# Middle tokens' output made transposed, and last block's slots 8, 9 and 11 through the common block routine

## The chip, the cores and the metric

One NeuronCore of a Trainium2 chip runs the whole kernel in one launch. The metric is the device time in microseconds (us) of one execution; the time of a kernel is the median of several executions. Engines: TensorE (PE in the profile; PEld is its weight load), VectorE (DVE), ScalarE (ACT), GpSimd (POOL), and SyncE (SP), which here only issues DMAs. PSUM is the memory that TensorE writes; DVE and ACT read it, in banks of 128 partitions x 512 fp32.

## The reference

`x` is (8, 3072, 256): 8 batches of 3072 tokens with 256 features. Two Fourier transforms (over tokens, over features), the real part, then a feed-forward layer with a maximum of three projections:

```python
X = np.fft.fft(x, axis=1)
X = np.fft.fft(X, axis=2)
x = X.real.reshape(8 * 3072, 256)
h = np.maximum(np.maximum(x @ w1, x @ w2), x @ w3)      # 768 wide
out = h @ w_out                                         # (24576, 256), float32
```

## The kernel before

**What is computed together.** The real part of the transform of a real sequence has a symmetry: token n and its mirror token 3072 - n are made of the same two parts, an even one `tE` and an odd one `tO`, by their sum and difference. So the kernel computes `tE` and `tO` (bf16, features on partitions) for half of the tokens, 1536 per batch, and makes two outputs of each: "plus" and "minus". Token 1536 is its own mirror; these 8 middle tokens, one per batch, are kept in `t_mid` (128 features x 2 parts x 8).

**The feed-forward part.** `max(a, b, c) = a + max(0, b - a, c - a)`. The term `a` is linear, so its product with `w_out` is folded into one small matrix `gw`: columns 0 to 255 for the even part, 256 to 511 for the odd one, 512 a marker column, and 514 to 769 the odd one with the signs of the mirrored half. Layer 1 (`unit_plus`, `unit_minus`, `unit_out`) makes the hidden values `hp` (plus) and `hm` (minus), 768 wide, as 6 chunks `jc` of 128; layer 2 multiplies them by `wout_bf`.

**Tiles and stages.** A batch has 3 blocks of 512 half tokens; a block is 6 layer-1 units (one per `jc`) and 4 slots of 128 half tokens, so a batch has slots 0 to 11. Partition p of slot s is the token with row r + 24p, r = s + 1, and its mirror is row 24 - r - 24p counted from the end. Slot 11 (r = 12) is its own partner row and needs special ranges.

**Order.** All engine orders are written out by hand (a manual schedule): the order of the calls is the order on each engine. Layer 1 of a block runs beside layer 2 of the block before: `l2_some(n)` takes n steps of the generator at the head of `l2_queue`, some 9 matmuls per unit. Behind each unit `l2_odd` is called for a slot whose line is ready, if fewer than two banks are in use.

**Layer 2 of an ordinary block** (`l2_even`, `l2_odd`, `l2_block`, lines 623 to 691). `l2_even` makes the even products of two slots in one PSUM bank `pl` (L629) and ScalarE copies them to an SBUF tile `even` (L632); the dictionary `lines` holds, for each slot, its part of `even`. `l2_odd` makes the odd product in a bank `po` (L640; pool `ps_o` has two such banks), DVE computes `other` from it (L643), the odd part with its sign turned, and POOL adds it to the even part (L646), which gives the line of the minus half. `odd` holds the bank, `banks` the slots in use. `l2_block` then accumulates 6 hidden products for plus and 6 for minus on the same bank (`l2_hidden`, L616), pops the slot's `lines` and `odd` before that, and adds line and bank on DVE (L670) into an output tile `ot` (4 buffers). Two slots share one `ot` up to slot 9. The minus half goes out by an indirect DMA from POOL (L677, rows from the table `rows_m`), since its rows run backwards; the plus half by a DMA from SP (L689).

**Layer 2 of the very last block** (batch 7, slots 8 to 11; `l2_last`, lines 693 to 728). There both halves are made from scratch: for each of the slots 11, 8, 9, 10 and each half, an even product (L711), an odd product (L713) and 6 hidden products, 16 matmuls per slot. The minus half uses tokens turned round, so that its rows run forwards and plain stores suffice: POOL turns `tE` and `tO` into `tEr` and `tOr` (L909, 512 columns each), and DVE writes the last block's `hm` backwards (`finish`, L891 to 894). DVE copies each bank out (L719, or L717 by halves for slot 10). Ten stores follow: nine from SP and one from ScalarE's queue (L727).

**Middle tokens** (`l2_mid`, lines 730 to 759). It runs beside block 0 of batch 7, five steps per unit. Layer 1 uses `t_mid` as 8 moving columns (L739, L741), layer 2 as 8 stationary columns: two products with `gw` (L752) and six with `wout_bf` (L616), each 256 columns wide, into 8 partitions of a bank `pom`; DVE copies 8 x 256 (L757) and SP stores 8 rows of 1 KB (L758).

Of the kernel before, what the change touches and what calls it, by code (L numbers as in the profile page):

```python
# [33 lines left out]
def kernel(  # L34
# [585 lines left out]
    odd = {}  # L620
    banks = set()

    def l2_even(b, slot):

        pl = ps_f.tile([128, 512], FP32, name="pl", tag="ps")
        for i in range(2):
            ci = (slot + i) * 128
            yield
            nc.tensor.matmul(pl[:, i * 256:(i + 1) * 256], mixes[b].tE[:, ci:ci + 128],  # L629
                             gw[:, 0:256], start=True, stop=True)  # L630
        even = even_pool.tile([128, 1024], FP32, name="even", tag="even")
        nc.scalar.copy(out=even.rearrange("p (i c) -> p i c", i=2)[:, :, 0:256],  # L632
                       in_=pl.rearrange("p (i c) -> p i c", i=2))
        for i in range(2):
            lines[b, slot + i] = even[:, i * 512:(i + 1) * 512]

    def l2_odd(b, slot):
# [12 lines left out]
    def l2_block(b, blk, hp, hm):  # L650

        base = b * S
        for sub in range(4):
            slot = blk * 4 + sub
            r = slot + 1
            sp = slice(sub * 128, sub * 128 + 128)
            if sub % 2:
                after = (b, slot + 1) if slot < 11 else (b + 1, 0)
                if after < (B - 1, 8):
                    yield from l2_even(*after)  # L660
            lin = lines.pop((b, slot))
# [8 lines left out]
            nc.vector.tensor_tensor(out=parts, in0=po.rearrange("p (i c) -> p i c", i=2),  # L670
                                    in1=lin.rearrange("p (i c) -> p i c", i=2), op=ALU.add)
            banks.remove((b, slot))
            if pair and not sub % 2:
                continue
            place = b * 7 + (slot // 2 if pair else slot - 5)
            wide = 512 if pair else 256
            stored(nc.gpsimd.indirect_dma_start(  # L677
                out.rearrange("(n two) c -> n (two c)", two=2) if pair else out,
                bass.IndirectOffsetOnAxis(ap=rows_m[:, place: place + 1], axis=0),
                ot[:, wide:2 * wide], None), "scattered", ("scattered", "direct"))  # L680
            nc.gpsimd.memset(mark, 0.0)
            if pair:
                stores = [(0, 128, base + r - 1)]
            elif r == 11:
                stores = [(0, 128, base + r)]
            else:
                stores = [(1, 64, base + 24), (64, 128, base + 12)]
            for (p0, p1, row) in stores:
                stored(nc.sync.dma_start(  # L689
                    out=bass.AP(out.tensor, out.offset + row * 256, [[24 * 256, p1 - p0], [1, wide]]),  # L690
                    in_=ot[p0:p1, 0:wide]), "direct", ("scattered",))

    def l2_last(hp, hm, te, to, flipped):

        base = (B - 1) * S
        ter, tor = flipped
        for sub in (3, 0, 1, 2):
            slot = 8 + sub
            r = slot + 1
            cp = slice(slot * 128, slot * 128 + 128)  # L700
            sp = slice(sub * 128, sub * 128 + 128)
            sm = slice((3 - sub) * 128, (4 - sub) * 128)
            po = ps_o.tile([128, 512], FP32, name="po", tag="po")
            ot = out_pool.tile([128, 1024], FP32, name="ot", tag="ot")
            for (h, tev, tov, wo, hid) in (
                    (0, te[:, cp], to[:, cp], gw[:, 256:512], lambda jc: hp[:, jc, sp]),
                    (1, ter[:, sm], tor[:, sm], gw[:, 514:770], lambda jc: hm[:, jc, sm])):
                if sub == 2 and h == 1:
                    po = ps_f.tile([128, 512], FP32, name="pol", tag="ps")
                ph = po[:, h * 256:(h + 1) * 256]  # L710
                nc.tensor.matmul(ph, tev, gw[:, 0:256], start=True, stop=False)  # L711
                yield
                nc.tensor.matmul(ph, tov, wo, start=False, stop=True)  # L713
                yield
                yield from l2_hidden(ph, hid)
                if sub == 2:
                    nc.vector.tensor_copy(out=ot[:, h * 256:(h + 1) * 256], in_=ph)  # L717
            if sub != 2:
                nc.vector.tensor_copy(out=ot[:, 0:512], in_=po)  # L719
            if r <= 11:  # L720
                stores = [(0, 128, base + r, 0), (0, 128, base + 24 - r, 256)]
            else:
                stores = [(0, 64, base, 0), (64, 128, base + 12, 0),
                          (0, 64, base + 1548, 256), (64, 127, base + 1560, 256)]
            for k, (p0, p1, row, c) in enumerate(stores):
                eng = nc.scalar if sub == 2 and k == 0 else nc.sync
                stored(eng.dma_start(out=out[row: row + 24 * (p1 - p0 - 1) + 1: 24, :],  # L727
                                     in_=ot[p0:p1, c:c + 256]), "direct", ("scattered",))

    def l2_mid():  # L730

        hmid = h_pool.tile([128, NJC, B], BF16, name="hmid", tag="hmid")
        n = NJC * B
        psm = ps_f.tile([128, 512], FP32, name="psm", tag="ps")
        for i in range(2):
            for jc in range(NJC):
                js = slice(jc * 128, (jc + 1) * 128)
                cs = slice(i * n + jc * B, i * n + (jc + 1) * B)
                nc.tensor.matmul(psm[:, cs], gE[i][:, js], t_mid[:, 0, :],  # L739
                                 start=True, stop=False)  # L740
                nc.tensor.matmul(psm[:, cs], gO[i][:, js], t_mid[:, 1, :],  # L741
                                 start=False, stop=True)
                yield
        stmp = h_pool.tile([128, TOKB + 16], BF16, name="stmp", tag="stmp")
        nc.scalar.activation(out=stmp[:, 0:n], in_=psm[:, 0:n], func=AX.Relu)
        nc.vector.tensor_tensor(out=hmid.rearrange("p jc n -> p (jc n)"), in0=psm[:, n:2 * n],
                                in1=stmp[:, 0:n], op=ALU.max)
        po = ps_f.tile([128, 512], FP32, name="pom", tag="ps")
        for _ in range(6):
            yield  # L750
        for k in range(2):
            nc.tensor.matmul(po[0:B, 0:256], t_mid[:, k, :], gw[:, k * 256:(k + 1) * 256],  # L752
                             start=(k == 0), stop=(k == 1))
            yield
        yield from l2_hidden(po[0:B, 0:256], lambda jc: hmid[:, jc, :])
        ot = out_pool.tile([128, 1024], FP32, name="ot", tag="ot")
        nc.vector.tensor_copy(out=ot[0:B, 0:256], in_=po[0:B, 0:256])  # L757
        stored(nc.sync.dma_start(out=out[NHALF: NHALF + S * (B - 1) + 1: S, :],  # L758
                                 in_=ot[0:B, 0:256]), "direct", ("scattered",))

    l2_queue = []

# [123 lines left out]
    for b in range(B):  # L886
# [4 lines left out]
        def finish(prev):  # L891
            pses, to, jc, hm = prev
            unit_minus(pses, to, jc)
            unit_out(pses, hm[:, jc, ::-1] if hm is last_hm else hm[:, jc, :], TOKB)

        last_hm = None
        if b == B - 1:
            flipped = []
            for t, name in ((tE, "tEr"), (tO, "tOr")):
                fl = h_pool.tile([128, TOKB], BF16, name=name, tag=name)  # L900
                flipped.append(fl)
        for blk in range(3):
            cs = slice(blk * TOKB, (blk + 1) * TOKB)
            hp = h_pool.tile([128, NJC, TOKB], BF16, name="hp", tag="hp")
            hm = h_pool.tile([128, NJC, TOKB], BF16, name="hm", tag="hm")
            if b == B - 1 and blk == 2:
                last_hm = hm
                for t, fl in zip((tE, tO), flipped):
                    nc.gpsimd.tensor_copy(fl, t[:, 3 * TOKB - 1: 2 * TOKB - 1: -1])  # L909
            for jc in range(NJC):  # L910
                pses = unit_plus(tE[:, cs], tO[:, cs], jc, TOKB)
                unit_out(pses, hp[:, jc, :], TOKB)
# [15 lines left out]
            l2_some(1000)  # L928
            if blk == 2:
                finish(prev)  # L930
            l2_queue.append(l2_last(hp, hm, tE, tO, flipped) if b == B - 1 and blk == 2 else
                            l2_block(b, blk, hp, hm))

    l2_some(1000)

# [28 lines left out]
```

## Time and profile before

| what | value |
|---|---|
| time, median of 3 runs (lowest, highest) | 405.08 us (404.48, 406.48) |
| profiled execution: its time | 406.24 us |
| profiled execution: span, first to last instruction | 404.5 us |
| granted TensorE clock | 1.00 in all 40 slices |
| hidden products L616, `hp` and `hm` | 1146 records, 171.2 us |
| layer-1 matmuls L591, L592, L599 | 816 records, 287.2 us |
| DVE add L670 | 92, mean 682 ns |
| DVE `other` L643 | 92, mean 476 ns |
| POOL add of even and other L646 | 92, mean 764 ns |
| POOL indirect store L677 | 53, mean 1018 ns |
| hardware queue q1 | 101976 packets, 42.21 MB, 41.9% of 16 DMA engines' span |

How to read it: the span is a little shorter than the time of the same execution, since it leaves out what lies before the first and behind the last instruction. A line of the timeline gives start, duration, engine, line of the code, operation, output <- inputs with their shapes, how many were merged, and in brackets how long the engine had been idle and what released it. Matmul durations overlap: a row of six matmuls of 0.273 us each takes 0.82 us. "SPq" and "ACTq" are DMA issues.

### The profile page before, as it was taken

How to read it: one execution, taken by the hardware profiler on the slowest of the kernel's cores; microseconds unless marked ns; L12 is line 12 of the kernel's file. 1: busy time of each engine (PE TensorE's matmuls, PEld its weight loads, DVE VectorE, ACT ScalarE, POOL GpSimd, SP SyncE). 2: the span in 40 equal slices, each digit the busy share in tenths (PEclk: the TensorE clock that was granted, in tenths of full speed). 3: DMA queues.
4: the chain of work that ended last, by engine and by line, in shares of the span. 5: the costliest groups of instructions: out<-in, count | busy, mean ns of one | idle time of the engine just before them, and what ended most of it. 6: DMA issues, size and time to landing. Idle time of an engine off the chain costs nothing.

```text
span 404.5 us, 8566 instructions
## 1 busy us (share of the span) xinstructions
PE 387.4 (96%) x2832; PEld 261.1 (65%) x2880; DVE 309.7 (77%) x556; ACT 265.5 (66%) x489; POOL 291.9 (72%) x394
## 2 busy tenths in 40 slices
PE   0999999999999999999999999999999999999996
PEld 0455677766676666766667666766677676666665
DVE  8798776787776886787777887778777877678884
ACT  6778667656766567666766676666766577655550
POOL 9589879879987898778967898768967623323521
PEclk9999999999999999999999999999999999999999
DMA  9999797689778848786489818886234411211214
GB/s 116 209 167 184 153 231 195 156 213 191 197 184 213 195 126 206 200 180 180 119 199 217 191 68 211 211 180 192 74 111 111 124 55 64 94 52 54 105 55 156
DMA packets 127598, 62.06 MB, mean 153 GB/s; under 512 B 111617, under 2 KB 116737, under 8 KB 126977
## 3 DMA queue, kind: packets, MB, share of 16 engines
q1 hardware_dynamic: 101976, 42.21, 41.9%
q0 software_dynamic: 24640, 18.98, 22.9%
q8 instruction: 22, 0.36, 0.4%
q10 hardware_dynamic: 936, 0.33, 0.3%
q14 instruction: 24, 0.19, 0.2%
HBM read 33.74 MB, written 29.88 MB: 157 GB/s over the span
## 4 chain that ended last, share of the span: by engine, by line
PE 88%; DVE 6%; issue 3%; ACT 2%; DVEq 0%; POOL 0%; ACTq 0%; POOLq 0%
PE po L616 29%; PE pse L591 16%; PE pse L599 14%; PE pse L592 12%; PE ps L571 3%; PE ps L573 3%; PE po L640 3%; PE pl L629 2%; PE warm L773 2%; PE ps L547 2%; DVE hm L606 2%; ACT stmp L605 2%; DVE other L643 1%; DVE ot L670 1%; PE psw L509 0%
## 5 line engine op out<-in xcount | busy, mean ns | idle before, releaser
L605 ACT ACTIVATE stmp<-pse 128x512 bf16<-128x512 f32 x288 | 170.7, 600 | 52.6 <-PE pse L592 26.1
L606 DVE TENSOR_TENSOR hp<-pse,stmp 128x512 bf16<-128x512 f32 x144 | 99.5, 691 | 80.3 <-ACT stmp L605 52.4
L646 POOL TENSOR_TENSOR even<-even,other 128x256 f32<-128x256 f32 x92 | 70.3, 764 | 76.3 <-DVE other L643 76.0
L591 PE MATMUL pse<-t,gE 128*128 128x512 bf16 x288 | 109.2, 379 | 2.6 <-DVE gD L488 0.2
L606 DVE TENSOR_TENSOR hm<-pse,stmp 128x512 bf16<-128x512 f32 x144 | 99.1, 689 | 3.3 <-ACT stmp L605 3.1
L592 PE MATMUL pse<-t,gO 128*128 128x512 bf16 x249 | 94.3, 379 | 0.0
L616 PE MATMUL po<-wout_bf,hp 128*128 128x256 bf16 x576 | 85.9, 272 | 0.0
L616 PE MATMUL po<-wout_bf,hm 128*128 128x256 bf16 x570 | 85.3, 273 | 0.3
L599 PE MATMUL pse<-t,gD 128*128 128x512 bf16 x279 | 83.7, 379 | 0.1
L677 POOL DMA_INDIRECT out_dram<-ot,rows_m x53 | 54.0, 1018 | 20.1 <-DVE ot L670 10.7
L616 PEld LDWEIGHTS <-hp 128*128 128x128 bf16 x576 | 56.3, 98 | 17.3 <-issue 2.5
L616 PEld LDWEIGHTS <-hm 128*128 128x128 bf16 x576 | 56.3, 98 | 16.6
L670 DVE TENSOR_TENSOR ot<-po,even 128x512 f32<-128x512 f32 x92 | 62.7, 682 | 0.0
L172 POOL CAST xw<-xs 96x544 bf16<-96x544 f32 (+1 forms) x48 | 53.3, 1122 | 0.0
L177 POOL CAST xb<-xs 96x512 bf16<-96x512 f32 x48 | 52.6, 1101 | 0.0
L575 ACT CAST t<-ps 128x512 bf16<-128x512 f32 x48 | 27.9, 586 | 34.8 <-PE ps L573 34.7
L599 PEld LDWEIGHTS <-gD 128*128 128x128 bf16 x288 | 28.1, 98 | 32.2
L643 DVE SCALAR_TENSOR_TENSOR other<-twice,po 128x256 f32<-128x256 f32 x92 | 43.8, 476 | 0.1
L591 PEld LDWEIGHTS <-gE 128*128 128x128 bf16 x288 | 28.2, 98 | 20.1 <-issue 0.7
L592 PEld LDWEIGHTS <-gO 128*128 128x128 bf16 x288 | 28.1, 98 | 20.1 <-issue 1.8
L552 ACT CAST z_all<-ps 128x480 bf16<-128x480 f32 x46 | 24.8, 560 | 23.2 <-PE ps L547 23.1
L632 ACT COPY even<-pl 128x512 f32<-128x512 f32 x46 | 27.0, 588 | 9.7 <-PE pl L629 8.6
(178 smaller groups left out, 373.3 us busy)
## 6 DMA issues: line engine op xcount, KB each, us to landing
xs<-in_x_dram SPq DMA_DIRECT2D x84, 198.0 KB
out_dram<-ot SPq DMA_DIRECT2D x39, 256.0 KB
xs<-in_x_dram SPq DMA_DIRECT2D x28, 192.0 KB
held<-xb SPq DMA_DIRECT2D x48, 96.0 KB
xw<-held POOLq DMA_DIRECT2D x24, 192.0 KB
raw_w<-in_moe_w_dram SPq DMA_DIRECT2D x4, 384.0 KB
out_dram<-ot SPq DMA_DIRECT2D x12, 128.0 KB
x<-in_x_dram POOLq DMA_DIRECT2D x8, 120.0 KB
```

Source lines behind the costliest of these rows:

```text
L172: nc.gpsimd.tensor_copy(v[:, d0:d1, ch * 32:ch * 32 + 32], xs[:, 0:32 * 64].rearrange("p (bb dl) -> p dl bb", dl=64)[:, d0:d1, :])
L177: nc.gpsimd.tensor_copy(mir[:, d0:d1, c0:c0 + 32], bass.AP(xs.tensor, xs.offset + 33 * 64 - 1 - d0, [xs.ap[0], [-1, d1 - d0], [-64, 32]]))
L591: nc.tensor.matmul(pse[:, 0:n], gE[i][:, js], te, start=True, stop=False)
L592: nc.tensor.matmul(pse[:, 0:n], gO[i][:, js], to, start=False, stop=True)
L599: nc.tensor.matmul(pse, gD[i][:, js], to, start=False, stop=True, skip_group_check=True)
L605: nc.scalar.activation(out=stmp[:, 0:n], in_=pses[0][:, 0:n], func=AX.Relu)
L606: nc.vector.tensor_tensor(out=dst, in0=src3, in1=stmp[:, 0:n], op=ALU.max)
L616: nc.tensor.matmul(po, hcols(jc), wout_bf[:, jc * 256:(jc + 1) * 256], start=False, stop=(jc == NJC - 1), skip_group_check=True)
L643: nc.vector.scalar_tensor_tensor(out=other, in0=twice, scalar=po[:, 256:257], in1=po[:, 0:256], op0=ALU.mult, op1=ALU.subtract)
L646: nc.gpsimd.tensor_tensor(out=line[:, 256:512], in0=line[:, 0:256], in1=other, op=ALU.add)
L670: nc.vector.tensor_tensor(out=parts, in0=po.rearrange("p (i c) -> p i c", i=2), in1=lin.rearrange("p (i c) -> p i c", i=2), op=ALU.add)
L677: stored(nc.gpsimd.indirect_dma_start(out.rearrange("(n two) c -> n (two c)", two=2) if pair else out, bass.IndirectOffsetOnAxis(ap=rows_m ...
```

## The change

Three parts.

- `l2_mid`: layer 2 uses `gw` and `wout_bf` as stationary (128 columns) and the 8 tokens as moving columns, in two halves of the 256 features: 16 matmuls into `pom` (128 features x 16). DVE copies 128 x 16. Two DMAs store it, each with 128 x 8 runs of one element.
- The last block goes through `l2_block` for slots 8, 9 and 11, with `l2_even` (slot 11 alone by `which=(1,)`), `l2_odd` called from inside the loop, and indirect stores for the minus half. `l2_last` is left with slot 10.
- Only slot 10 is turned round: two copies of 128 columns of `tE`, `tO` into `tEr`, and behind each unit of the last block one copy of 128 columns of `hm` by POOL, into `tOr` (chunks 0 to 3) or `tEr` (chunks 4, 5). `hm` itself is written forwards.

```diff
-    def l2_even(b, slot):
+    def l2_even(b, slot, which=(0, 1)):
         pl = ps_f.tile([128, 512], FP32, name="pl", tag="ps")
-        for i in range(2):
+        for i in which:
...
-        nc.scalar.copy(out=even.rearrange("p (i c) -> p i c", i=2)[:, :, 0:256],
-                       in_=pl.rearrange("p (i c) -> p i c", i=2))
-        for i in range(2):
+        i0, i1 = which[0], which[-1] + 1
+        nc.scalar.copy(out=even.rearrange("p (i c) -> p i c", i=2)[:, i0:i1, 0:256],
+                       in_=pl.rearrange("p (i c) -> p i c", i=2)[:, i0:i1, :])
+        for i in which:
             lines[b, slot + i] = even[:, i * 512:(i + 1) * 512]
...
     def l2_block(b, blk, hp, hm):
         base = b * S
-        for sub in range(4):
+        at_end = (b, blk) == (B - 1, 2)
+        for sub in (0, 1, 3) if at_end else range(4):
             slot = blk * 4 + sub
+            for more in (slot, slot + 1 if sub < 1 else 11) if at_end else ():
+                if (b, more) in lines and len(banks) < 2:
+                    l2_odd(b, more)
             r = slot + 1
...
                 after = (b, slot + 1) if slot < 11 else (b + 1, 0)
-                if after < (B - 1, 8):
+                if after < (B - 1, 10):
                     yield from l2_even(*after)
+                elif after == (B - 1, 10):
+                    yield from l2_even(*after, (1,))
             lin = lines.pop((b, slot))
             po = odd.pop((b, slot))
...
-    def l2_last(hp, hm, te, to, flipped):
+    def l2_last(hp, te, to, flipped):
         base = (B - 1) * S
-        ter, tor = flipped
-        for sub in (3, 0, 1, 2):
...
+        ter, tor, hidden_r = flipped
+        cp = slice(10 * 128, 11 * 128)
+        ot = out_pool.tile([128, 1024], FP32, name="ot", tag="ot")
+        for (h, tev, tov, wo, hid) in (
+                (0, te[:, cp], to[:, cp], gw[:, 256:512], lambda jc: hp[:, jc, 256:384]),
+                (1, ter, tor, gw[:, 514:770], hidden_r)):
+            pool, name, tag = ((ps_o, "po", "po"), (ps_f, "pol", "ps"))[h]
+            po = pool.tile([128, 512], FP32, name=name, tag=tag)
+            ph = po[:, 0:256]
+            nc.tensor.matmul(ph, tev, gw[:, 0:256], start=True, stop=False)
+            yield
+            nc.tensor.matmul(ph, tov, wo, start=False, stop=True)
+            yield
+            yield from l2_hidden(ph, hid)
+            nc.vector.tensor_copy(out=ot[:, h * 256:(h + 1) * 256], in_=ph)
+        for (eng, row, c) in ((nc.scalar, base + 11, 0), (nc.sync, base + 13, 256)):
+            stored(eng.dma_start(out=out[row: row + 24 * 127 + 1: 24, :], in_=ot[:, c:c + 256]),
+                   "direct", ("scattered",))
...
     def l2_mid():
...
-        for k in range(2):
-            nc.tensor.matmul(po[0:B, 0:256], t_mid[:, k, :], gw[:, k * 256:(k + 1) * 256],
-                             start=(k == 0), stop=(k == 1))
-            yield
-        yield from l2_hidden(po[0:B, 0:256], lambda jc: hmid[:, jc, :])
+        for half in range(2):
+            to_bank = po[:, half * B:(half + 1) * B]
+            for k in range(2):
+                c = k * 256 + half * 128
+                nc.tensor.matmul(to_bank, gw[:, c:c + 128], t_mid[:, k, :],
+                                 start=(k == 0), stop=False)
+            for jc in range(NJC):
+                c = jc * 256 + half * 128
+                nc.tensor.matmul(to_bank, wout_bf[:, c:c + 128], hmid[:, jc, :],
+                                 start=False, stop=(jc == NJC - 1))
+                if jc % 2:
+                    yield
         ot = out_pool.tile([128, 1024], FP32, name="ot", tag="ot")
-        nc.vector.tensor_copy(out=ot[0:B, 0:256], in_=po[0:B, 0:256])
-        stored(nc.sync.dma_start(out=out[NHALF: NHALF + S * (B - 1) + 1: S, :],
-                                 in_=ot[0:B, 0:256]), "direct", ("scattered",))
+        nc.vector.tensor_copy(out=ot[:, 0:2 * B], in_=po[:, 0:2 * B])
+        for half in range(2):
+            stored(nc.sync.dma_start(
+                out=bass.AP(out.tensor, out.offset + NHALF * 256 + half * 128,
+                            [[1, 128], [S * 256, B], [1, 1]]),
+                in_=ot[:, half * B:(half + 1) * B].unsqueeze(2)), "direct", ("scattered",))
...
         def finish(prev):
             pses, to, jc, hm = prev
             unit_minus(pses, to, jc)
-            unit_out(pses, hm[:, jc, ::-1] if hm is last_hm else hm[:, jc, :], TOKB)
+            unit_out(pses, hm[:, jc, :], TOKB)
+            if hm is last_hm:
+                nc.gpsimd.tensor_copy(last_hidden(jc), hm[:, jc, 383:255:-1])
+
+        def last_hidden(jc):
+            t, c = (flipped[1], jc * 128) if jc < 4 else (flipped[0], (jc - 2) * 128)
+            return t[:, c:c + 128]
...
-                for t, fl in zip((tE, tO), flipped):
-                    nc.gpsimd.tensor_copy(fl, t[:, 3 * TOKB - 1: 2 * TOKB - 1: -1])
+                for i, t in enumerate((tE, tO)):
+                    nc.gpsimd.tensor_copy(flipped[0][:, i * 128:(i + 1) * 128],
+                                          t[:, 11 * 128 - 1: 10 * 128 - 1: -1])
...
-            l2_queue.append(l2_last(hp, hm, tE, tO, flipped) if b == B - 1 and blk == 2 else
-                            l2_block(b, blk, hp, hm))
+            l2_queue.append(l2_block(b, blk, hp, hm))
+    l2_queue.append(l2_last(hp, tE, tO, (flipped[0][:, 0:128], flipped[0][:, 128:256], last_hidden)))
```

More of the change, by code (lines that the diff above doesn't have):

```diff
@@ L691, in l2_block @@
                     in_=ot[p0:p1, 0:wide]), "direct", ("scattered",))
-    def l2_last(hp, hm, te, to, flipped):
+    def l2_last(hp, te, to, flipped):
         base = (B - 1) * S
-        ter, tor = flipped
-        for sub in (3, 0, 1, 2):
[L698 to L711, printed above, removed]
-                yield
[L713 to L728, printed above, removed]
@@ L750, in l2_mid @@
             yield
-        for k in range(2):
-            nc.tensor.matmul(po[0:B, 0:256], t_mid[:, k, :], gw[:, k * 256:(k + 1) * 256],
-                             start=(k == 0), stop=(k == 1))
-            yield
-        yield from l2_hidden(po[0:B, 0:256], lambda jc: hmid[:, jc, :])
-        ot = out_pool.tile([128, 1024], FP32, name="ot", tag="ot")
-        nc.vector.tensor_copy(out=ot[0:B, 0:256], in_=po[0:B, 0:256])
-        stored(nc.sync.dma_start(out=out[NHALF: NHALF + S * (B - 1) + 1: S, :],
-                                 in_=ot[0:B, 0:256]), "direct", ("scattered",))
+        for half in range(2):
[10 more added lines that the diff above has]
+                    yield
+        ot = out_pool.tile([128, 1024], FP32, name="ot", tag="ot")
+        nc.vector.tensor_copy(out=ot[:, 0:2 * B], in_=po[:, 0:2 * B])
[4 more added lines that the diff above has]
+                in_=ot[:, half * B:(half + 1) * B].unsqueeze(2)), "direct", ("scattered",))
     l2_queue = []
@@ L898 @@
             flipped = []
-            for t, name in ((tE, "tEr"), (tO, "tOr")):
-                fl = h_pool.tile([128, TOKB], BF16, name=name, tag=name)
-                flipped.append(fl)
+            for name in ("tEr", "tOr"):
+                flipped.append(h_pool.tile([128, TOKB], BF16, name=name, tag=name))
         for blk in range(3):
```

## The prediction

> **What bounds the kernel now.** I read the page first: busy shares, then the chain that ended last.
>
> ```profile
> span 404.5 us, 8566 instructions
> PE 387.4 (96%) x2832; PEld 261.1 (65%) x2880; DVE 309.7 (77%) x556; ACT 265.5 (66%) x489; POOL 291.9 (72%) x394
> PE 88%; DVE 6%; issue 3%; ACT 2%; DVEq 0%; POOL 0%; ACTq 0%; POOLq 0%
> ```
>
> TensorE is busy 96% of the span and is 88% of the chain, so a matmul removed anywhere in the middle is a gain, as long as TensorE gets no new wait. The change touches two places, so I then read busy time by window around both.
>
> ```profile
> 360.00:368.00 8.00, 7.95 (x51) 4.39 (x51) 6.04 (x12) 4.17 (x7) 3.49 (x7) 1.00 0.23 90
> 384.00:394.16 10.16, 10.05 (x67) 6.56 (x67) 8.75 (x15) 5.75 (x11) 3.17 (x5) 1.00 0.14 56
> 394.16:402.00 7.84, 7.15 (x65) 6.16 (x63) 4.34 (x8) 0.58 (x1) 1.08 (x2) 1.00 0.48 166
> ```
>
> The columns are length, then busy time of PE, PEld, DVE, ACT and POOL, the clock, DMA share and GB/s. The first row holds the middle tokens' output: PE 7.95 of 8.00. The last is the tail (`l2_last`): TensorE runs without a break to its last matmul while DVE has 3.5 us and POOL 6.8 us free. The tail has cover on DVE and POOL, but only if TensorE need not wait for them.
>
> **Middle tokens: removed and added.** The timeline of the middle tokens:
>
> ```profile
> 352.71 0.17 PE L739 MATMUL psm<-t_mid,gE 128*128 128x8 bf16 x1
> 352.73 0.17 PE L741 MATMUL psm<-t_mid,gO 128*128 128x8 bf16 x1
> ...
> 359.72 0.49 PE L616 MATMUL po<-wout_bf,hm 128*128 128x256 bf16 x3
> 360.14 0.09 PEld L752 LDWEIGHTS <-t_mid 128*8 128x8 bf16 x2 [0.21 <-issue]
> 360.14 0.38 PE L752 MATMUL pom<-gw,t_mid 128*8 128x256 bf16 x2
> 360.45 0.10 PEld L591 LDWEIGHTS <-gE 128*128 128x128 bf16 x1 [0.22 <-issue]
> ```
>
> A matmul of 256 columns takes a slot of 0.109 us (six in one row take 0.82, of which 0.273 is the first). Eight go: 8 x 0.109 = 0.87. The 8-column weight loads also break the stream: from L616 at 359.72 to the next L591 at 360.45 are 0.73 us for five matmuls worth 0.545, 0.18 lost; the other two clusters (362.31 to 363.37 and 365.00 to 366.07, eight matmuls each) lose 0.19 and 0.20. Removed: 0.87 + 0.57 = 1.44. Added are 16 matmuls of 128x128 weights by 8 columns. Just this shape is in the trace: the starts of L739 and L741 are 0.025 apart, without a gap behind them. 16 x 0.025 = 0.40. TensorE is the bound there, so **-1.04 us**. From both sides: +0.13 if each cost a full weight load of 0.098 (16 x 0.098 = 1.57), -1.44 if they vanished; I take the row of the same shape.
>
> The Trainium skill speaks against this edit: its page "TensorE: Matmul & The Clock Gate", section "LDWEIGHTS (loading the stationary operand)", puts a load at its columns / 1.2 ns, so it is the stationary operand's columns that cost. By that 16 loads of 128 columns would be 1.7 us and the edit +0.3 (an estimate from that page). The 0.025 us between starts in L739/L741 does not agree, and the row decides.
>
> Its store goes from one of 8 x 1 KB to two of 1024 runs of 4 bytes each on SP's queue; rival C prices it. Until then I cost it at nothing: as built, its buffer is next wanted by the add of slot 4 of the last batch, at 385.01, some 20 us after the store.
>
> **The tail: work.** Before, 4 slots x 16 = 64 matmuls of 256 columns. After, slots 8, 9 and 11 need 1 even + 1 odd + 12 hidden, slot 10 still 16. That would be 58. But the order of the changed program has six odd products L641, not three: slot 8 once in the last unit and again in `l2_block`, slot 9 twice, slot 11 twice. The reason is in the code: the new loop asks `(b, more) in lines`, and a line is popped only afterwards, so a slot already done passes the test again. Hence 61 matmuls: -3 x 0.109 = -0.33. Three of them (even of 8 and 9, first odd of 8) now lie ahead of the last L599 pair, whose slots end at 394.16 + 0.33 = 394.49.
>
> **The tail: waits.** The price is not the repeated matmul. Two banks hold `po`, and each repeat takes the bank of the slot before, so in the order of the changed program TensorE waits (1) for DVE's add of the slot before, then (2) for DVE's `other`, which must read the odd product before the hidden products accumulate on it. Behind that waiting matmul everything else on TensorE is queued. Rows:
>
> ```profile
> 393.69 0.69 DVE L606 TENSOR_TENSOR hm<-pse,stmp 128x512 bf16<-128x512 f32 x1
> 393.73 0.59 PE L599 MATMUL pse<-t,gD 128*128 128x512 bf16 x2
> 394.30 0.68 DVE L670 TENSOR_TENSOR ot<-po,even 128x512 f32<-128x512 f32 x1
> 394.90 0.68 DVE L606 TENSOR_TENSOR hm<-pse,stmp 128x512 bf16<-128x512 f32 x1
> 400.49 0.82 PE L616 MATMUL pol<-wout_bf,hm 128*128 128x256 bf16 x6
> 401.35 0.42 DVE L717 COPY ot<-pol 128x256 f32<-128x256 f32 x1 [0.45 <-PE pol L616]
> ```
>
> `other` takes 0.48 (0.40 from its start to the next start, 387.28 to 387.68). TensorE starts 0.05 after DVE ends (22.76 + 1.92 = 24.68, L480 at 24.73); DVE starts 0.04 after a matmul's end. In times of this trace, the middle's gain left out:
> - Slot 7's add: hm at 393.69, then the new `other` at 394.30, the add at 394.70, end 395.38. TensorE, ready at 394.49, waits to 395.43 (0.94).
> - Slot 8: DVE still has the last hm (395.30) ahead of `other` (395.90 to 396.38). Hidden products start at 396.43, slots end 12 x 0.109 later at 397.74, results 0.16 later; add 397.94 to 398.62.
> - From add to add: 0.05 + odd matmul 0.27 + 0.04 + `other` 0.48 + 0.05 + hidden 1.47 + 0.04 + add 0.68 = 3.08. Slot 9's add ends at 401.70.
> - Slot 11: hidden products start at 401.70 + 0.89 = 402.59, slots end 403.90.
> - Slot 10 waits for no bank: 16 x 0.109 = 1.74 to 405.64, results 405.80, copy to 406.24 against 401.77 before.
>
> So the tail is **+4.47 us**: some 4.8 of waits less 0.33 of matmuls.
>
> Hidden beside it: POOL flips eight tiles of 128 columns in place of two of 512 (0.62 each); a small one is between 0.09 (its 1x1 memset) and 0.62, and POOL is busy 3.17 of 10.16 us in the last block, so nothing; were that cover gone, at most eight times the upper end less 1.23, 3.7 us, on POOL's queue. ScalarE's new even copy (0.59) lies in its 1.03 us idle before 392.41. The last hm is written forwards at 0.69 (393.69) and backwards at 0.68 (394.90): nothing. Slot 11's line on POOL stands behind an indirect store: 401.70 + 0.15 + 0.99 + 0.09 + 2 x 0.73 = 404.40, after its matmuls (404.06) but ahead of slot 10's copy, so nothing.
>
> **Sum.** 4.47 - 1.04 = +3.43: span 404.5 to 407.9. The profiled execution took 406.24, 1.16 above the median of 405.08; the difference goes on the median: 405.08 + 3.43 = 408.5 us, +0.85%.
>
> **Rivals.**
> A (not slower): TensorE doesn't wait, because the repeats find banks and DVE free early. For: DVE is busy 4.34 of 7.84 us in the tail, and the page shows no TensorE wait in the last block. Against: the order has an explicit wait for DVE ahead of each hidden group in the repeats, and DVE must finish the slot before. It decides if all waits together come under 1.4 us in place of 4.8. All hidden: 405.08 - 0.33 - 1.04 = 403.7.
> B: the middle gains nothing, the narrow matmuls being bound by weight loads (0.098 each, +0.13): 405.08 + 4.47 + 0.13 = 409.7. Against: L739/L741. The skill's rule above would land here, at 409.8.
> C: the 4-byte stores clog SP's queue and the rings, later stores land late, DVE waits for an output buffer. The nearest issue is an x load of 768 to 792 runs, median 1.01 us, longest 4.05: 1.3 to 5.3 each for 1024. The hardware queue's packets average 0.419 x 16 x 404.5 / 101976 = 26.6 ns of one engine, 2048 / 16 x 26.6 = 3.4 us. 2.6 to 10.6 plus 3.4 is under the 20 us of cover. It decides from about 150 ns a packet (19 us); at 200 ns (26 us) some 6 us late, 414. "DMA: Bandwidth & Descriptors", section "Specifications", of the Trainium skill says writes under 512 B are read-modify-write; no run here shows what 4 bytes cost.
> D: the end is slot 11's indirect store, not slot 10's. POOL issues it at about 405.3, done 406.3, level with slot 10's last copy (406.24), from which the span runs 2.73 more (401.77 to 404.5). If an indirect store lands 1 us slower than a direct one: 409.5. The trace shows no landing times.
>
> **Chances.** Forecast 72%, D 10%, A 8%, B 7%, C 3%. The forecast's own spread: four latency chains of some 0.1 to 0.2 each, and a median of three runs that lie 2 us apart; 407.2 to 409.6. Taking in B and most of D, and a middle gain of up to 1.44, 8 in 10 lie in 406.9 to 410.0. About 0.5% (2.0 us) is what a measurement can tell from no change. Slower by more than that (over 407.1): nearly all of the forecast, B, C and D, 86%. Same: most of A and the low end of the forecast, 10%. Faster: 4%.
>
> **What would show it.** Six L641 matmuls for slots 8, 9 and 11; in the tail three pairs of TensorE waits of 0.6 to 0.9 us released by DVE's add and by `other`; add to add 3.1 us; the last DVE copy ends some 3.4 us later than at 401.77. In the middle 16 matmuls 0.025 apart and no gap around them. I am wrong if the tail's waits sum to under 3 us, if the narrow matmuls stand 0.05 us apart or more, or if DVE waits for an output buffer near 385.

## The result and the profile after

| | before | after |
|---|---|---|
| time, median of 6 runs each on one chip (lowest, highest) | 405.28 us (404.48, 406.48) | 424.76 us (420.90, 426.92) |
| ratio, 95% interval | | 1.0476 [1.0441, 1.0511] |
| profiled execution: its time, its span | 406.24, 404.5 us | 425.97, 424.2 us |

Slower, by 19.5 us where 3.4 were forecast. The page of the changed kernel (span; busy time by engine; the granted clock, in tenths, in 40 slices; the chain that ended last):

```profile
span 424.2 us, 8607 instructions
PE 391.4 (92%) x2837; PEld 262.4 (62%) x2885; DVE 312.0 (74%) x562; ACT 266.1 (63%) x491; POOL 300.2 (71%) x410
PEclk9999999999999999999999999999999999987998
...
PE 78%; DVE 7%; DMA 6%; issue 3%; ACT 3%; POOL 1%; POOLq 0%; DVEq 0%; ACTq 0%
```

TensorE has hardly more to do (391.4 us for 387.4, part of it at a lower clock), but it falls from 96% to 92% of the span, and DMA, absent from the chain before, is 6% of it. So the loss is waiting, and some of it is waiting for transfers. The windows of the changed kernel show where (columns: stretch, its length, busy time with instruction counts of PE, PEld, DVE, ACT and POOL, the clock, the DMA engines' share, GB/s; a transfer's packet counts whole in the stretch in which it begins, so the share can pass 1):

```profile
360.00:368.00 8.00, 7.89 (x64) 5.11 (x63) 6.62 (x13) 4.29 (x8) 3.86 (x9) 1.00 0.72 78
368.00:376.00 8.00, 3.46 (x18) 1.73 (x16) 1.89 (x3) 2.15 (x4) 0.60 (x1) 0.85 1.21 18
376.00:384.00 8.00, 7.08 (x44) 4.38 (x44) 5.05 (x9) 3.35 (x6) 2.53 (x4) 0.94 1.01 40
384.00:394.00 10.00, 6.69 (x26) 3.39 (x25) 4.64 (x9) 2.39 (x4) 2.26 (x5) 0.66 0.49 87
...
410.00:418.00 8.00, 5.27 (x44) 4.03 (x42) 4.01 (x8) 0.37 (x1) 4.47 (x7) 1.00 0.18 72
418.00:424.20 6.20, 0.00 (x0) 0.00 (x0) 0.06 (x1) 0.00 (x0) 0.42 (x2) 0.77 0.24 81
```

From 368 to 376 us the DMA share is 1.21 at 18 GB/s, where the first 100 us have 1.03 at 181 GB/s: the DMA engines are full and move nearly nothing, and every engine of the core is busy less than half of that time. In the kernel before, the same stretch has TensorE busy for 7.95 of 8 us at a DMA share of 0.19:

```profile
368.00:376.00 8.00, 7.95 (x54) 5.19 (x54) 7.00 (x13) 4.17 (x7) 2.99 (x6) 1.00 0.19 64
```

In the changed kernel the clock falls too (0.85, 0.94, then 0.66). The last row is the second surprise: 6 us in which nothing computes.

Start times in the two traces divide the 19.7 us between the spans. The first middle matmul is the anchor, because executions differ by some 2 us before it: it starts at 352.50 before, at 352.29 after, and between 350.26 and 352.44 in the kernels below (pool_late apart, which is told there).

| stretch | before | after | difference |
|---|---|---|---|
| start to first middle matmul (L739; L731 after) | 352.50 | 352.29 | -0.21 |
| from there to one and the same L591 behind them (368.46; 367.25) | 15.96 | 14.96 | -1.00 |
| from there to the last L599 pair (393.73; 406.15) | 25.27 | 38.90 | +13.63 |
| last L599 pair to the end of the last DVE copy (401.77; 418.06) | 8.04 | 11.91 | +3.87 |
| last copy to the end of the span | 2.73 | 6.14 | +3.41 |

Of the 13.63, 0.33 are the three tail matmuls moved ahead of that pair; 13.3 are a stall. The timeline of the middle matmuls in the changed kernel (start, duration, engine, line, operation):

```profile
359.83 0.20 PE L747 MATMUL pom<-t_mid,gw 128*128 128x8 bf16 x2
359.89 0.24 PE L751 MATMUL pom<-hmid,wout_bf 128*128 128x8 bf16 x4
359.99 0.81 PE L591 MATMUL pse<-t,gE 128*128 128x512 bf16 x2
```

Six matmuls in 0.16 us and no gap behind them, as forecast. The same view a few us later:

```profile
363.64 2.82 SPq L758 DMA_DIRECT2D out_dram<-ot  x2
...
373.58 0.60 ACT L605 ACTIVATE stmp<-pse 128x512 bf16<-128x512 f32 x1 [5.11 <-remote]
373.62 0.69 DVE L606 TENSOR_TENSOR hp<-pse,stmp 128x512 bf16<-128x512 f32 x1 [5.83 <-remote]
...
374.23 0.58 PE L591 MATMUL pse<-t,gE 128*128 128x512 bf16 x1 [4.54 <-ACT stmp L605]
...
387.74 0.69 DVE L677 TENSOR_TENSOR ot<-po,even 128x512 f32<-128x512 f32 x1 [3.40 <-DMA out_dram<-ot,rows_m]
...
388.49 0.37 PE L641 MATMUL po<-gw,t 128*128 128x257 bf16 x1 [3.07 <-DVE ot L677]
```

The two stores of single elements are issued at 363.64. VectorE stops 4 us later (5.83 us until 373.62), then ScalarE and TensorE. At 384 VectorE waits 3.4 us for the store out of its output buffer, and TensorE 3.07 us for VectorE. That store is not one of the two: it is GpSimd's indirect store (`rows_m`) of the slots before, issued at 363.46; by the semaphore updates in the trace it landed at 387.55, 24 us after its issue, where the same one in the kernel before took 2.4 us (363.94 to 366.35). The second of the two 4-byte stores landed at 390.80, 27 us after its issue at 364.07. The matmul at 374.23 takes 0.58 us where it took 0.38: the clock has fallen during the pause.

### The profile page after: what moved, and what is told of

It is laid out like the page before. It is cut to its first block, busy times and chain, and to the rows that moved or that the text cites. A ratio compares the mean times of both kernels' runs of the same rounds, so it can differ in the third digit from the quotient of the medians.

```text
span 424.2 us, 8607 instructions
## 1 busy us (share of the span) xinstructions
PE 391.4 (92%) x2837; PEld 262.4 (62%) x2885; DVE 312.0 (74%) x562; ACT 266.1 (63%) x491; POOL 300.2 (71%) x410
## 4 chain that ended last, share of the span: by engine, by line
PE 78%; DVE 7%; DMA 6%; issue 3%; ACT 3%; POOL 1%; POOLq 0%; DVEq 0%; ACTq 0%
PE po L616 25%; PE pse L591 14%; PE pse L599 13%; PE pse L592 11%; DMA out_dram<-ot,rows_m 6%; PE ps L571 2%; PE ps L573 2%; PE po L641 2%; PE pl L629 2%; PE warm L775 2%; PE ps L547 2%; ACT stmp L605 2%; DVE hm L606 2%; DVE other L644 1%; DVE ot L677 1%
## 5 line engine op out<-in xcount | busy, mean ns | idle before, releaser
L647 POOL TENSOR_TENSOR even<-even,other 128x256 f32<-128x256 f32 x98 | 74.6, 761 | 85.5 <-DVE other L644 84.6
L591 PE MATMUL pse<-t,gE 128*128 128x512 bf16 x288 | 110.1, 382 | 8.2 <-ACT stmp L605 5.4
L592 PE MATMUL pse<-t,gO 128*128 128x512 bf16 x249 | 95.3, 383 | 0.0
L616 PE MATMUL po<-wout_bf,hp 128*128 128x256 bf16 x576 | 86.8, 274 | 2.3 <-DVE other L644 2.3
L599 PE MATMUL pse<-t,gD 128*128 128x512 bf16 x279 | 84.6, 383 | 0.1
L677 DVE TENSOR_TENSOR ot<-po,even 128x512 f32<-128x512 f32 x95 | 64.9, 683 | 8.9 <-DMA out_dram<-ot,rows_m 3.4
L684 POOL DMA_INDIRECT out_dram<-ot,rows_m x55 | 55.9, 1017 | 18.9 <-DVE ot L677 7.4
L599 PEld LDWEIGHTS <-gD 128*128 128x128 bf16 x288 | 28.3, 98 | 32.9 <-issue 1.1
L644 DVE SCALAR_TENSOR_TENSOR other<-twice,po 128x256 f32<-128x256 f32 x98 | 46.6, 476 | 0.1
L592 PEld LDWEIGHTS <-gO 128*128 128x128 bf16 x288 | 28.2, 98 | 26.6 <-issue 8.6
L591 PEld LDWEIGHTS <-gE 128*128 128x128 bf16 x288 | 28.4, 99 | 19.8 <-DVE gD L488 0.6
L633 ACT COPY even<-pl 128x512 f32<-128x512 f32 (+1 forms) x48 | 28.0, 583 | 12.9 <-PE pl L629 11.7
```

What stands on the lines that cost most here:

```text
L591: nc.tensor.matmul(pse[:, 0:n], gE[i][:, js], te, start=True, stop=False)
L592: nc.tensor.matmul(pse[:, 0:n], gO[i][:, js], to, start=False, stop=True)
L599: nc.tensor.matmul(pse, gD[i][:, js], to, start=False, stop=True, skip_group_check=True)
L616: nc.tensor.matmul(po, hcols(jc), wout_bf[:, jc * 256:(jc + 1) * 256], start=False, stop=(jc == NJC - 1), skip_group_check=True)
L644: nc.vector.scalar_tensor_tensor(out=other, in0=twice, scalar=po[:, 256:257], in1=po[:, 0:256], op0=ALU.mult, op1=ALU.subtract)
L647: nc.gpsimd.tensor_tensor(out=line[:, 256:512], in0=line[:, 0:256], in1=other, op=ALU.add)
```

## Experiments

Times are medians. The runs were made on three chips, each with the kernel before beside them, and differences are against that: 404.61 us for mid_old, mid_only, own_line and tail_once; 405.42 for shared_aside, line_64, half_store and pool_late; 405.20 for mid_turned, pool_late2, shared_pitch and to_sbuf. Lines left out of a code cut are marked by `...`.

### The two parts apart

**mid_old**: the changed kernel with the old layer 2 of the middle tokens, so the tail alone.

```diff
+        for k in range(2):
+            nc.tensor.matmul(po[0:B, 0:256], t_mid[:, k, :], gw[:, k * 256:(k + 1) * 256],
+                             start=(k == 0), stop=(k == 1))
+            yield
+        yield from l2_hidden(po[0:B, 0:256], lambda jc: hmid[:, jc, :])
...
```

> The changed kernel with the middle tokens' output and store put back as before; the tail stays changed. Theory 1 (two causes: the 4-byte stores cost some 16 us, the tail's waits some 4.2): before 405.3 + 4.2, near 409.5, span near 408.7, and no stop of all engines behind 364 us. Theory 2 (the long stop comes from the new tail's POOL work and indirect stores): stays near 424. The tail itself, from the end of the last layer-1 pair to DVE's last copy, is 11.5 us in both.

**mid_only**: the kernel before with the `l2_mid` part of the change's diff, and nothing else of it.

> The kernel before with the new middle tokens' output and its 4-byte stores alone. Theory 1: 405.3 - 1.0 + 16.3, near 420.5, with the same stop of all engines from about 369 to 374 us. Theory 2: 404.3, a little faster than before.

Measured: mid_old 412.86 us, ratio 1.0196 [1.0177, 1.0214], +8.25; mid_only 415.17 us, 1.0261 [1.0237, 1.0285], +10.6. Both parts lose; together 18.8 of the 19.5. mid_only has the same stall: its window from 368 to 376 has a DMA share of 1.52 at 11 GB/s. And the tail loses nearly twice the 4.47 us that were forecast for it. mid_only lies 5.3 us under its expectation, whose 16.3 us for the stores held the late end of the program too; its stall is also a little shorter, 11.9 us in its trace (first middle matmul to the last L599 pair: 52.11 us, against 40.23 in mid_turned, which has the same matmuls) in place of 13.3.

### What about the stores stalls the core

Six kernels leave the matmuls of the changed kernel as they are and change only where the elements go, or how many of them. Five send them elsewhere and so leave the middle tokens' rows of the output unwritten; half_store leaves half of each row unwritten.

**own_line**: each element of 4 bytes to a 512-byte line of its own.

```diff
...
+            aside = aside_pool.tile([128, 1024], FP32, name="aside", tag="aside")
+            dst = aside.rearrange("p (n c) -> p n c", n=B)[:, :, 0:1]
+            nc.sync.dma_start(out=dst, in_=ot[:, half * B:(half + 1) * B].unsqueeze(2))
...
```

> The changed kernel, but the middle tokens' 2048 elements of 4 bytes go to a scratch tensor in DRAM, each to a 512-byte line of its own, so the middle tokens' rows of the output are left out. Theory 1a (the cost lies in many writers meeting in one line: in the changed kernel 128 neighbouring elements share 512 bytes): the clog is gone or a small part, near 410. [...]

Measured: 410.99 us, 1.0151 [1.0133, 1.017], +6.4. The windows of own_line:

```profile
360.00:368.00 8.00, 7.95 (x62) 5.21 (x62) 6.76 (x13) 4.75 (x8) 3.57 (x6) 1.00 0.33 69
368.00:376.00 8.00, 7.95 (x52) 4.99 (x52) 6.59 (x12) 4.97 (x9) 2.51 (x4) 1.00 0.17 66
```

As many runs of 4 bytes, on the same queue at the same place, and no trace of a stall: TensorE is at 7.95 of 8.00 throughout, the DMA share is back at 0.17 by 368. Were each write of 4 bytes dear by itself, own_line would have stayed as long as the changed kernel. So neither the number of runs nor their size is the price. The packets in the traces show where the full share comes from. From 363 to 392 us the 4-byte packets of the hardware queue take 44 ns on the mean in the changed kernel (2137 packets, in all 5.9 us of the 16 engines' time) and 8 ns in own_line (1969 packets, 0.9 us). The other packets beside them lengthen more: those of 4 KB and more of GpSimd's queue take 1140 ns on the mean against 165, the longest 13.8 us.

**shared_aside**: to scratch, in the pattern of the output (128 neighbouring elements of 4 bytes, each from another partition, fill 512 bytes of a row), rows 1 KB apart. **line_64**: elements 64 bytes apart, so that 8 share 512 bytes.

```diff
...
+            dst = bass.AP(aside.tensor, aside.offset, [[1, 128], [256, B], [1, 1]])       # shared_aside
+            dst = bass.AP(aside.tensor, aside.offset, [[16, 128], [128 * 16, B], [1, 1]]) # line_64
...
```

> The changed kernel; the middle tokens' 2048 elements go to a small scratch tensor in DRAM in the same pattern as in the output (128 neighbours of 4 bytes share 512 bytes), so the middle tokens' rows of the output are left out. Theory 1a (neighbouring writers sharing a line cost): as the changed kernel, 420 to 427, with the stop of the engines. Rival 1c (it is the output tensor or the 3 MB step between its middle rows that costs): as with own lines, near 411.

> As shared_aside, but each 4-byte element 64 bytes from the next, so eight share 512 bytes and none shares 64; the middle tokens' rows of the output are left out. If the unit that writers must share to cost is 64 bytes or less: near 411, as with own lines of 512 bytes. If it is 512 bytes: slower than 411, up to 424.

**half_store**: only one of the two stores of the changed kernel.

```diff
-        for half in range(2):
+        for half in range(1):
```

> The changed kernel with only the first of the two 4-byte stores; the upper 128 features of the middle tokens' rows are left out. If the clog goes with the number of writes: half of the 13 to 14 us, near 418. If it has a cover of some 10 us (buffers and work already released) before anything waits: near 411 to 413.

Measured: shared_aside 417.89 us, 1.0319 [1.0281, 1.0356]; line_64 411.29 us, 1.015 [1.0122, 1.0177]; half_store 418.15 us, 1.0322 [1.0293, 1.035]. The windows from 368 to 376 us of shared_aside and of line_64:

```profile
368.00:376.00 8.00, 7.40 (x50) 4.68 (x48) 5.21 (x9) 3.29 (x6) 2.52 (x4) 1.00 0.95 17
368.00:376.00 8.00, 8.00 (x53) 4.98 (x52) 6.93 (x12) 4.93 (x9) 2.52 (x4) 1.00 0.17 66
```

Elements side by side in DRAM bring a stall back, though they go to scratch, and 64 bytes of distance take it away with only their addresses changed. Eight elements to 512 bytes thus cost nothing that shows. The simplest reading is that writers must not share a piece of 64 bytes or less. It isn't shown: line_64 also puts fewer elements into 512 bytes (8 in place of 128), and no distance between 4 and 64 bytes was tried in DRAM. Half of the elements cost about half: +12.7 where all cost +19.5 and harmless stores +6.1 (mean of own_line, line_64 and to_sbuf).

**shared_pitch**: as shared_aside, but rows 3 MB apart, as in the output. **to_sbuf**: the elements 8 bytes apart in an SBUF tile.

```diff
...
+            dst = bass.AP(aside.tensor, aside.offset + half * 128, [[1, 128], [S * 256, B], [1, 1]])  # shared_pitch
+                out=w_high[:, half * 16:half * 16 + 16].rearrange("p (n c) -> p n c", c=2)[:, :, 0:1], # to_sbuf
...
```

> As shared_aside, but the scratch rows lie 3 MB apart, as the middle rows of the output do; the middle tokens' rows of the output are left out. shared_aside (rows 1 KB apart) took 417.9, the changed kernel 424.8, own lines 411.0. If the step between the rows makes the rest of the loss: near 424. If it is that other stores to the output run beside: near 418.

> The changed kernel; the 2048 elements of 4 bytes go to SBUF, 8 bytes apart, 8 in each partition, so 64 bytes are shared by 8 elements of one partition; the middle tokens' rows of the output are left out. If sharing costs in DRAM alone: as own lines, near 411. If sharing costs wherever the target is: up to 418 or more.

Measured: shared_pitch 421.12 us, 1.0404 [1.0381, 1.0427]; to_sbuf 411.31 us, 1.0156 [1.0134, 1.0179]. In SBUF eight neighbours within 64 bytes cost nothing that shows; in DRAM sixteen do (those in SBUF come from one partition, those in DRAM from several, and eight were not tried in DRAM). The distance of the rows seems to explain part of what shared_aside lacks of the changed kernel (medians 417.9, 421.1 and 424.8), but the runs overlap: shared_aside's reach up to 419.69, shared_pitch's lie from 417.67 to 421.67, the changed kernel's from 420.90. The rest, 3.6 us, stays open; what differs still is that the elements go into the tensor that all other stores write.

### The narrow matmuls with another store

**mid_turned**: the kernel before with the narrow matmuls; VectorE turns the 128 x 32 result in blocks of 32 x 32, and four stores write runs of 128 bytes.

```diff
...
+        nc.vector.memset(ot[:, 2 * B:32], 0.0)
+        nc.vector.tensor_copy(out=ot[:, 0:2 * B], in_=po[:, 0:2 * B])
+        turned_mid = h_pool.tile([128, 32], FP32, name="turned_mid", tag="turned_mid")
+        nc.vector.transpose(out=turned_mid, in_=ot[:, 0:32])
+        for g in range(4):
+            stored(nc.sync.dma_start(
+                out=bass.AP(out.tensor, out.offset + NHALF * 256 + g * 32,
+                            [[128, 2], [S * 256, B], [1, 32]]),
+                in_=turned_mid[g * 32:g * 32 + 2 * B, :]), "direct", ("scattered",))
```

> The kernel before with the narrow middle matmuls; DVE turns the 128 x 16 result in 32 x 32 squares and four stores of 16 runs of 128 bytes take it out, each run to lines of its own. Theory 1 (the narrow matmuls save 1.04 us of TensorE and the store was the whole loss): 405.3 - 1.0, near 404.2, no stop behind 364 us. Rival (the saving is lost in the end, or the extra DVE work of about 0.4 us shows): 405.3.

Measured: 404.74 us (12 runs), ratio 0.9993 [0.9979, 1.0006]: no difference that shows, where -1.0 was expected. The timeline of mid_turned:

```profile
362.22 0.21 DVE L767 STREAM_TRANSPOSE turned_mid<-ot 128x32 f32<-128x32 f32 x1
...
362.56 2.68 SPq L769 DMA_DIRECT2D out_dram<-turned_mid  x4
```

From the first middle matmul to the last L599 pair it takes 40.23 us (351.20 to 391.43), before 41.23 (352.50 to 393.73). So the 1.00 us is there in the trace, and no stall. From the last copy to the end of the span it takes 3.0 us in place of 2.73, and the start scatters by more than the gain. A gain of 0.7 to 0.8 lies within the interval (-0.85 to +0.24 us); that it reaches the median wasn't shown. No version that was run beats the kernel before.

### The tail: repeats and the end

**tail_once**: mid_old, and an odd product is not asked for twice.

```diff
-                if (b, more) in lines and len(banks) < 2:
+                if (b, more) in lines and (b, more) not in odd and len(banks) < 2:
```

> Middle tokens as before; the tail as changed, but l2_odd is not called again for a slot whose odd product is already there: 58 matmuls instead of 61, and no bank is taken a second time. Theory 1 (the repeats cost by the waits that they bring): one wait of some 0.9 us ahead of slot 8, one of some 1.3 ahead of slot 11, in all +1.5 on before: near 406.8, so 2.7 less than with the repeats. Theory 2 (a repeat costs its matmul alone): 0.33 less than with the repeats, near 409.2.

Measured: 409.80 us, 1.0133 [1.0103, 1.0163]: 3.06 us under mid_old, but +5.2 against before and 3.0 above what was expected. From the last L599 pair to the end of the last copy it takes 9.28 us (392.61 to 401.89), mid_old 11.90: the repeats cost 2.6. The last copy thus ends level with that of before (401.77), and yet the span is 407.9: 6.0 us lie behind that copy, where before had 2.73. This is the second loss, and it has nothing to do with the repeats. Behind its last work GpSimd runs three DRAIN instructions, one long and two short. The trace of the kernel before has them so (count; shortest, median and longest in ns; first and last start), and that of mid_old:

```profile
L959 POOLq DRAIN  x3: 46/103/6292, 395.0 to 404.2; - x3
```

```profile
L957 POOLq DRAIN  x3: 46/103/6292, 403.9 to 410.7; - x3
```

The long one is the first: before 395.0 to 401.3, some 5.0 us behind POOL's last instruction (ended 396.33), over before the last stores land (403.48 by the semaphore updates in the trace). In mid_old it runs from 403.9 to 410.2, again 5.0 behind POOL's last (405.22), with nothing beside it: the last stores had landed at 407.1.

**pool_late** and **pool_late2**: the kernel before, with one small GpSimd copy behind the last copy of VectorE, into a new tile of 4 bytes a partition (pool_late) or into one that is there (pool_late2). No store is changed.

```diff
+    late_mark = consts.tile([128, 1], FP32, tag="late_mark")         # pool_late
...
+            if sub == 2:
+                nc.gpsimd.tensor_copy(late_mark, ot[:, 511:512])      # pool_late
+                nc.gpsimd.tensor_copy(dif, ot[:, 511:512])            # pool_late2
```

> The kernel before, and POOL copies one column of 128 elements behind the last DVE copy, with no DMA from POOL after 396 us. Theory 3 (POOL's final drain ends 5.0 us after its last instruction of any kind, and the program ends 0.8 behind it): last copy 401.8 + 0.3 + 5.0 + 0.8 = span 407.9, so +3.4, near 408.4. Rival 3b (the drain follows only a recent indirect store from POOL): no change, 405.

> As pool_late, but POOL's one column goes to a tile that is already there, so no tile of SBUF moves. pool_late lost some 17 us in its first 100 us, where its added tile of 4 bytes had moved every later tile. Theory 3 (the program waits for a POOL drain of 4.4 to 5 us behind POOL's last instruction, whatever it is) and the moved tiles as the cause of the rest: span 401.8 + 0.4 + 4.4 + 0.8 = 407.4, near 408.2. Rival (the copy itself costs the rest): 425 as pool_late.

Measured: pool_late 427.17 us, 1.0556 [1.05, 1.0611]; pool_late2 408.08 us, 1.0068 [1.0045, 1.0091]. In pool_late2 POOL's copy ends at 401.96, and then:

```profile
L961 POOLq DRAIN  x3: 46/103/4632, 401.8 to 406.9; - x3
```

The drain ends at 406.4, 4.4 behind the copy, and the span at 407.2, with the last stores landed at 403.4. One copy of 0.19 us without any store costs 2.9 us because it moves POOL's last instruction from 396.3 to 402.0. So it is the drain, not the landing of an indirect store: the last of these landed at 397.9 here.

pool_late was meant to show this and shows something else besides: its drain is as long (4.63 us), but most of its 21.8 us arise ahead of the tail. In its trace 15.3 us are lost before the first middle matmul (367.78 for 352.50), 11 of them in the first 95 us. Its page and its first 100 us:

```profile
q1 hardware_dynamic: 101976, 42.21, 51.9%
```

```profile
0.00:100.00 100.00, 80.64 (x578) 51.72 (x579) 69.44 (x149) 64.07 (x119) 72.98 (x93) 0.97 1.43 150
```

The queue moves the same packets and bytes as before, where they took 41.9% of 16 engines' span and TensorE was busy 88.28 us of the first 100. The new tile stands ahead of nearly all others, so it moves where they lie in SBUF. That the shift slows the transfers is argued from pool_late2, which has the same copy and not the tile; that alignment is the reason wasn't tried.

## Why the prediction was wrong, point by point

- **The sign and the two edits' own sizes were right.** Middle: -1.04 was forecast; from the first middle matmul to the same L591 are 14.96 us in the changed kernel, own_line, line_64, to_sbuf and mid_turned, and 15.96 in before, mid_old and tail_once: -1.00. Rival B (+0.13) is out: the row of the same shape, 0.025 us each, was the right price. The Trainium skill's page "TensorE: Matmul & The Clock Gate", section "LDWEIGHTS (loading the stationary operand)", puts a load at its columns / 1.2 ns, from which the prediction had +0.3 (an estimate). The traces don't bear out that price: the records of these loads are 0.10 us long, but they start 0.025 us apart.
- **The tail's waits were right**: +4.47 forecast, 0.33 + 3.87 = 4.20 measured. The changed kernel's timeline of the tail has the waits on VectorE's `other` and add that the prediction built up:

```profile
406.92 0.27 PE L641 MATMUL po<-gw,t 128*128 128x257 bf16 x1 [0.17 <-DVE other L644]
407.52 0.27 PE L641 MATMUL po<-gw,t 128*128 128x257 bf16 x1 [0.33 <-DVE ot L677]
...
408.51 0.81 PE L616 MATMUL po<-wout_bf,hp 128*128 128x256 bf16 x6 [0.72 <-DVE other L644]
...
411.21 0.81 PE L616 MATMUL po<-wout_bf,hp 128*128 128x256 bf16 x6 [1.01 <-DVE other L644]
...
413.54 0.27 PE L641 MATMUL po<-gw,t 128*128 128x257 bf16 x1 [0.74 <-DVE ot L677]
...
414.38 0.81 PE L616 MATMUL po<-wout_bf,hp 128*128 128x256 bf16 x6 [0.58 <-DVE other L644]
...
417.64 0.42 DVE L717 COPY ot<-pol 128x256 f32<-128x256 f32 x1 [0.24 <-PE pol L616]
```

TensorE's six waits sum to 3.55, and each of the six breaks loses some 0.16 more, the part of a matmul (0.27 less its slot of 0.109) that otherwise runs beside the next: 4.5, where some 4.8 were forecast. One place differs: the first repeat waited 0.17 us for `other`, and the product behind it 0.33 for slot 7's add, in place of 0.94. Rival A (waits under 1.4 us) is out.
- **The step that failed is the store's: "Until then I cost it at nothing".** It cost 13.3 us, and the case for it (rival C, 414 us) had 3%. The prediction priced the number of packets from rows of other transfers and asked how late the stores' own buffer would be. For 4-byte runs apart from each other that price was more than enough: in own_line they take 8 ns each for the 26.6 assumed and are gone by 368. What no row of the kernel before could show is that such writes side by side in DRAM lengthen the core's other transfers. The sign that the prediction named, VectorE waiting for an output buffer near 385, did come (384.34), but for the indirect store issued ahead of the two, whose landing took 24 us. Nor does that wait come first: the engines stop at 368, 16 us earlier, with their waits on TensorE's semaphore. Rival C was thus right in the clog and in the stores' lateness (26 us at its 200 ns a packet; 27 measured), but not in what it delays; and the lateness agrees by luck, since the 4-byte packets took 44 ns on the mean and not 200. The Trainium skill's page "DMA: Bandwidth & Descriptors", section "Specifications", calls writes under 512 B read-modify-write. By itself that would hold for own_line and line_64 as well, and these cost nothing that shows.
- **The second step that failed is the end**: the span was taken to run 2.73 us behind the last copy, as before. It ran 6.1. Rival D (10%) named the place, POOL's late indirect store, but its reason, a slow landing, is wrong: the trace's semaphore updates, which the prediction said weren't there, have slot 11's indirect store landed at 419.95 and the last plain one at 420.27, while the drain runs to 423.4. Where the prediction costs POOL's late work in the tail at "nothing", that was right for the work, but it overlooked that the program's end waits for POOL's drain.
- In sum: -1.0 + 4.2 + 3.4 + 13.3 = 19.9 against 19.5 between the medians.

**Open.** What stops VectorE and ScalarE at 368: TensorE had issued matmuls through 369.69, but the semaphore updates of its work from 366.44 on arrive only in a burst at 373.53 to 373.69, a gap of 7.1 us where the longest before is 1.85. ScalarE and VectorE wait for just this semaphore and start at 373.58 and 373.62. The gap falls within the clog; what holds these updates wasn't tried. The later waits for output buffers are plain in the timeline.

## What to carry to other kernels

Avoid a store that puts single elements from different partitions side by side in DRAM: transpose on chip first (0.2 us on VectorE here) and write runs. Price such a store not only by its own packets and its own buffer, but by what it may do to the transfers beside it. Price the end of a kernel by the last instruction of each engine, not by the last store alone: here work moved onto GpSimd late cost its drain. And before a call that makes something is put inside a loop, look whether it can run twice for the same item; here three repeated matmuls of 0.1 us cost 2.6 us of waits.

## What was not expected of the hardware

- 2048 writes of 4 bytes, 16 of them to each 64 bytes of the output in DRAM, cost 13.3 us, and in the same pattern in scratch some 6.6 to 9.8 more than harmless stores (417.89 and 421.12 us); at 64 bytes apart and more, or in SBUF, nothing shows (410.99 to 411.31 us in three kernels).
- Within the clog engines paused that waited for TensorE's semaphore and for no transfer (ScalarE 5.1 us, VectorE 5.8), and TensorE's granted clock fell to 0.66 in 384 to 394 us behind the pauses.
- GpSimd's long drain at the end of the program ends 4.4 us behind a small copy and 4.9 to 5.2 behind an indirect store with its memset, the two kinds of last work that were run.
- With a tile of 4 bytes a partition allocated early, the same packets took 51.9% in place of 41.9% of the DMA engines' span, and the kernel some 19 us more than its twin without the tile (427.17 and 408.08 us); why stays open.
